# Assigning tokens to tiles by contiguous row groups of x instead of one stride over all of x

## The chip, the cores and the metric

One core of a Trainium2 chip. The metric is the device time of one execution in microseconds (us), lower is better. A median stands for a series of executions; the profile is one further execution, and its span leaves out some 1.3 us of start and end that the time has. A load has landed when the last of its 16 DMA engines has reported. Runs come in two states: a run is called slow when it is over 1.5% above the fastest of its kernel, and only fast runs enter a ratio. All views below are of fast runs with a granted TensorE clock of 1.0 unless the text says otherwise.

## The reference, cut to what matters

```python
# x: [1, 2048, 448] bfloat16; wqkv [448, 1344]; w_phi [16, 28, 28]; wo [448, 448]; w1 [448, 1792]; w2 [1792, 448]
xn = layernorm(x)                       # per token
q, k, v = heads(xn @ wqkv)              # 16 heads of 28
phi_q, phi_k = hedgehog(q @ w_phi), hedgehog(k @ w_phi)   # softmax(+), softmax(-) side by side
attn = (phi_q @ (sum over tokens of phi_k x v)) / (phi_q @ sum of phi_k + 1e-6)
out = x + attn @ wo + silu(xn @ w1) @ w2
```

The 2,048 tokens meet only in the sums over tokens. So any assignment of tokens to the 16 tiles of 128 gives the same result, as long as the load of x and the store of the output agree.

## The kernel before

Five engines run one fixed program each. A small scheduler in the kernel orders it at build time from estimated durations; it looks at the on-chip side of each transfer only. The FFN is the feed-forward part (w1, silu, w2); an eviction copies a result of TensorE out of its accumulators. Parts (cuts marked):

```python
xt = A_x[0].rearrange("(p t) d -> p t d", p=128)      # partition p holds rows 16p .. 16p+15
outt = out[0].rearrange("(p t) d -> p t d", p=128)
...
def load_x(t0, t1):
    load(x_sb[:, t0:t1, :], xt[:, t0:t1, :], f"x{t0}", lat=1400.0)
...
load(Wp[:], ..., "wphi", eng="act")                   # 448 pieces of 56 bytes, ScalarE queue
...
load_x(0, 1); load_x(1, 2); load_x(2, 4)              # sync queue, in this order
load(w1_sb[:, 0:2, 0:512], ..., "w1_0")               # "the first w1 load" below
load(w1_sb[:, 2:4, 0:512], ..., "w1_0r")
load_w1(512, 1024, "act")                             # 384 KB on the ScalarE queue, 128 KB on the sync queue
load_x(4, 8); load_w1(1024, FF); load_rows4(wv_sb, ...)
load_x(8, 12); load_x(12, 16)
...
# the sync queue's order from tile 8 on; wT_dma0..7: transposing loads of the q/k weights from HBM,
# xnT_dma: on-chip transposes of normalised x
chain("x8 wT_dma0 wT_dma1 wT_dma2 x12 xnT_dma5 xnT_dma7 wT_dma3 wT_dma4 wT_dma5 wT_dma6 wT_dma7 xnT_dma9 ...".split())
# VectorE's fixed order of the layer norm: statistics, aggregate, reciprocal, normalise of tiles 0 to 3
chain("bnst0 bnag0 bnst1 bnag1 rstd0 xn0a xn0 rstd1 xn1 bnst2 bnag2 bnst3 bnag3 rstd2 xn2 rstd3 xn3 ev3".split())
# TensorE: transposes tr0, tr1, then FFN pieces of tile 0 ("00a 10a") and tile 1 ("01a 11a"), and so on
...
# the "fold": q/k weights (wT) times the feature weights (BDphi); it needs all eight wT loads
mms += [(wps[:, g, :], wT_sb[0:KP, qk * 4 + g, ...], BDphi[:, g, :], True, True) for g in range(G)]
...
P.dma(lambda e: e.dma_start(out=outt[:, t, cs], in_=res[:, cs]), ..., name="out_dma", ...)
```

The softmax here doesn't subtract the row's maximum and nothing guards it: scores larger than these inputs give would overflow.

Of the kernel before, what the change touches and what calls it, by code (L numbers as in the profile page):

```python
# [344 lines left out]
def bass_parallel_sum__linear_kernel_hedgehog__dense_activation_silu__prompt_kernel(  # L345
# [23 lines left out]
    EPS_DEN = 1e-6  # L369
    NYT = 4  # L370
    XN_DMA0 = 4
    xt = A_x[0].rearrange("(p t) d -> p t d", p=128)
    outt = out[0].rearrange("(p t) d -> p t d", p=128)

    es = contextlib.ExitStack()
    with es:
        def sb(name, shape, dt):
            return es.enter_context(nc.sbuf_tensor(name, shape, dt))

        x_sb = sb("x_sb", [128, NT, D], BF16)  # L380
# [57 lines left out]
        NOS = 4  # L438
# [12 lines left out]
        P = _Prog()  # L451
# [7 lines left out]
        def d_dve(n, mode=1, nptr=0):  # L459
            return n * 1.042 / mode + 160.0 + 30.0 * nptr  # L460
# [38 lines left out]
        def load(dst, src, name, eng="sp", lat=1700.0):  # L499
            n = 2  # L500
            for _, cnt in list(dst.ap):
                n *= cnt
            P.dma(lambda e: e.dma_start(out=dst, in_=src), n / 280.0, writes=[dst], name=name, eng=eng, lat=lat)  # L503
# [5 lines left out]
             reads=[ones_bf[:]], writes=[ident[:]], name="ident")  # L509
# [17 lines left out]
        for i in range(38):  # L527
            P.op("pe", 107.0, lambda e: e.matmul(banks[3][:, 0:128], ones_bf[:], ones_bf[:], start=True, stop=True),
                 reads=[ones_bf[:]], writes=[banks[3][:, 0:128]], name="warm", mode=128)
# [1 line left out]


        def load_x(t0, t1):
            load(x_sb[:, t0:t1, :], xt[:, t0:t1, :], f"x{t0}", lat=1400.0)

        def load_rows4(dst, src, c0, c1, name, eng="sp"):
            load(dst[:, 0:3, :], src[0:KF, c0:c1].rearrange("(k p) f -> p k f", p=128), name, eng)
# [2 lines left out]
        def load_w1(c0, c1, eng="sp"):  # L540
            load_rows4(w1_sb[:, :, c0:c1], B_w1, c0, c1, f"w1_{c0}", eng)

        load_x(0, 1)
        load_x(1, 2)
        load_x(2, 4)
        load(w1_sb[:, 0:2, 0:512], B_w1[0:256, 0:512].rearrange("(k p) f -> p k f", p=128), "w1_0")
        load(w1_sb[:, 2:4, 0:512], bass.AP(B_w1.tensor, B_w1.offset + 256 * FF, [[FF, 128], [64 * FF, 2], [1, 512]]), "w1_0r")
# [246 lines left out]
        ob_cnt = [0]  # L794
# [58 lines left out]
        def out_ev(t, ob, addend, cs):  # L853
            res = x_sb[:, t, :]
            P.op("dve", d_dve(cs.stop - cs.start), lambda e: e.tensor_tensor(res[:, cs], ob, addend[:, cs], ALU.add),  # L855
                 reads=[ob, addend[:, cs]], writes=[res[:, cs]], name="out_ev")
            P.dma(lambda e: e.dma_start(out=outt[:, t, cs], in_=res[:, cs]), 100.0, lat=1200.0, reads=[res[:, cs]], name="out_dma", out_slot=ob_cnt[0] % NOS,
                  eng="sp" if cs.start else "act")
            ob_cnt[0] += 1

# [3 lines left out]
        def finish_tile(t, q, bs):  # L864
            for b, cs in parts(bs):
                ob = banks[b][:, 0:cs.stop - cs.start]
                wo_fulls(q, ob, cs, False)
                P.cur_slack = 400.0
                pe_mms([wo_rem(q, ob, slice(0, 128), cs)], "wo_mm")
                P.cur_slack = 0.0  # L870
                out_ev(t, ob, addend(t), cs)

        def finish_tiles(tiles):
            cs = slice(0, D)
            rows = [[x for x in tiles if x[1] % 2 == i] for i in range(2)]
            tiles = [r[n] for n in range(max(map(len, rows))) for r in rows if n < len(r)]
            pe_mms([wo_rem(q, banks[b][:, 0:D], slice(64 * (q % 2), 64 * (q % 2) + 64), cs) for t, q, b in tiles], "wo_rem",
                   dur=d_mm(D) * max(map(len, rows)), mode=64)
            for t, q, b in tiles:
                out_ev(t, banks[b][:, 0:D], addend(t), cs)  # L880
# [23 lines left out]
        for word in "tr0a tr0 tr1 00a 10a 01a 11a 00b 10b 01b 11b tr2 20 21 tr3 02 12 22 03 13 23".split():  # L904
# [3 lines left out]
            f, t = int(word[0]), int(word[1])  # L908
# [42 lines left out]
        for word in PLAN.split():  # L951
            n0 = len(P.ops)
            kind, arg = word[0], word[1:]
            if kind == "a":
                t, b = map(int, arg[1:].split("@"))
                blocks[arg[0], t] = open_kind[arg[0]](t, b)
                blocks[arg[0], t][2](0)
            elif kind == "b":
                f = blocks[arg[0], int(arg[1:])]
# [5 lines left out]
            elif kind == "K":  # L965
                t0, t1 = map(int, arg.split("-"))
# [9 lines left out]
            elif kind == "U":  # L976
                t, _, b = arg.partition("@")
                att((int(t),), (int(b or UB),))
            elif kind in "FY":
                head, _, cnt = arg.partition(":")  # L980
                t, _, bs = head.partition("@")
                t = int(t)
                if bs:
                    bank_of[t] = [int(c) for c in bs]
                k = done.get(t, 0)
                done[t] = k + int(cnt) if cnt else FT
                if kind == "Y":
                    y_tile(t, bank_of[t][0], k, done[t])
                else:
                    ffn2(t, bank_of[t], False, k, done[t])  # L990
            elif kind == "W":
                t, _, b = arg.partition("@")
                t = int(t)
                if b:
                    bank_of[t] = [int(b)]
                wo_fulls(slot_of[t], banks[bank_of[t][0]][:, 0:D], slice(0, D), t in yts)
            elif kind == "R":
                finish_tiles([(t, slot_of[t], bank_of[t][0]) for t in map(int, arg.split(","))])
            elif kind == "E":
                t = int(arg)  # L1000
                finish_tile(t, slot_of[t], bank_of[t])
            else:
                assert kind == "r"
                t = int(arg)
                P.cur_slack = 400.0
                pe_mms([wo_rem(slot_of[t], banks[bank_of[t][0]][:, 0:D], slice(0, 128), slice(0, D))], "wo_mm")
                P.cur_slack = 0.0
                out_ev(t, banks[bank_of[t][0]][:, 0:D], addend(t), slice(0, D))
# [98 lines left out]
```

## Time and profile before

| | before |
|---|---|
| time, median of 3 | 149.47 us (149.24 to 149.51) |
| span of the profile | 148.2 us |
| TensorE busy | 143.6 us, 97% |
| first FFN matmul | 6.81 us |
| fold begins | 26.38 us |
| last matmul of all begins | 145.90 us |

The prediction below shows the busy shares, the chain, and the head of the timeline. The page also has the span in 40 slices (each 3.7 us; digits are busy tenths, the DMA row is the share of the 16 DMA engines):

```profile
PE   7799999999999999999999999999999999999994
...
DMA  4999955999500000000089570058788467532325
GB/s 101 370 381 211 298 98 97 189 226 347 140 2 4 0 0 7 4 0 4 0 159 168 102 141 4 0 101 172 151 108 176 86 91 144 150 103 51 60 68 184
```

The reader is to see that TensorE is full from the third slice on, and that the second and third slices, 3.7 to 11 us, move 370 to 381 GB/s. The lines of the timeline read:

```profile
6.81 1.81 PE L469 MATMUL psum<-xnT,phT 128*128 128x128 bf16 x24
7.55 0.90 PEld L469 LDWEIGHTS psum<-xnT,phT 128*128 128x128 bf16 x16 [0.31 <-ACT xnT L489]
8.46 0.39 PE L484 MATMUL psum<-ident,RA 128*128 128x128 bf16 x4
...
26.38 0.96 PE L469 MATMUL psum<-BDphi,Y_sb 112*128 112x112 bf16 x16
```

(start, duration, engine, line, operation, out<-in, shapes, count; in the bracket the idle time before it and what ended it). First come the FFN's first 24 matmuls, then the weight load (PEld) at which they pause 0.31 us for tile 1, then the third transpose. The last line is the fold.

### The profile page before, as it was taken

Reading aid. Unit: us, or ns where it says so; the run is one execution under the profiler, and the core shown is the slowest. Engines: PE = TensorE matmul, PEld = TensorE weight load, DVE = VectorE, ACT = ScalarE, POOL = GpSimd, SP = SyncE. Lnnn points to the kernel's source line nnn. Section 1 sums busy time; section 2 is a strip of 40 time slices with the busy share of each in tenths; the row PEclk is TensorE's granted clock in tenths of the full one; section 3 lists DMA queues with packets and bytes.
Section 4 is the critical chain, followed back from the end, with each engine's and each line's share of the span. In section 5 each row is a group of like instructions: output and inputs, shape, how many; then the busy total and the mean of one; then the engine's idle time right before and its main releaser. Section 6 shows DMA issues by size and latency. Waiting matters only on the chain.

```text
span 148.2 us, 3656 instructions
## 1 busy us (share of the span) xinstructions
PE 143.6 (97%) x1540; PEld 79.3 (53%) x1540; DVE 90.3 (61%) x189; ACT 70.7 (48%) x88; POOL 71.4 (48%) x82
## 2 busy tenths in 40 slices
PE   7799999999999999999999999999999999999994
PEld 7594444554554556646444444555545655455573
DVE  1878997541499949504995003999477802915284
ACT  4477757357999399979555859400012000000000
POOL 7108566510079999998799900799000800000000
DMA  4999955999500000000089570058788467532325
GB/s 101 370 381 211 298 98 97 189 226 347 140 2 4 0 0 7 4 0 4 0 159 168 102 141 4 0 101 172 151 108 176 86 91 144 150 103 51 60 68 184
DMA packets 44352, 17.42 MB, mean 117 GB/s; under 512 B 36912, under 2 KB 43952, under 8 KB 44336
## 3 DMA queue, kind: packets, MB, share of 16 engines
q1 hardware_dynamic: 41168, 14.99, 47.7%
q10 hardware_dynamic: 3168, 2.20, 4.8%
q8 instruction: 12, 0.20, 0.6%
q14 instruction: 4, 0.03, 0.1%
HBM read 6.56 MB, written 1.84 MB: 57 GB/s over the span
## 4 chain that ended last, share of the span: by engine, by line
PE 93%; DMA 2%; DVE 2%; ACT 0%; issue 0%; SPq 0%
PE psum L469 93%; DMA x_sb<-in_A_x_dram 2%; DVE RA L617 1%; PE psum L484 1%; DVE x_sb L855 1%; DVE st L602 0%; ACT xnT L489 0%; SPq L503 0%; DVE mv L603 0%; DVE rstd L608 0%
## 5 line engine op out<-in xcount | busy, mean ns | idle before, releaser
L469 PE MATMUL psum<-xnT,phT 64*128 64x512 bf16 (+1 forms) x428 | 45.7, 350 | 0.3
L469 PE MATMUL psum<-w_sb,hT 128*128 128x448 bf16 (+1 forms) x238 | 45.2, 342 | 0.0
L737 DVE TENSOR_REDUCE Rec<-Ek_sb 128x32 f32<-128x896 bf16 (+1 forms) x20 | 24.3, 1246 | 26.8 <-ACT Ek_sb L489 19.2
L773 POOL TENSOR_TENSOR RA<-Ek_sb,Rec 128x896 bf16<-128x896 bf16 x16 | 27.0, 1721 | 21.1 <-DVE Rec L738 19.7
L489 ACT ACTIVATE hT<-psum 128x1024 bf16<-128x1024 f32 x28 | 27.2, 1023 | 13.2 <-PE psum L469 13.2
L469 PEld LDWEIGHTS psum<-w_sb,hT 128*128 128x128 bf16 x238 | 22.3, 98 | 18.7 <-issue 1.5
L469 PEld LDWEIGHTS psum<-xnT,phT 64*128 64x128 bf16 (+1 forms) x428 | 20.8, 95 | 21.1 <-PE psum L469 1.7
L489 ACT ACTIVATE Ek_sb<-psum 128x864 bf16<-128x864 f32 x24 | 20.2, 933 | 17.4 <-DVE x_sb L855 16.1
L469 PE MATMUL psum<-Wqk,xnT 64*128 64x432 bf16 x224 | 23.7, 343 | 0.1
L747 POOL TENSOR_TENSOR Ek_sb<-Ek_sb,Rec 128x896 bf16<-128x896 bf16 x8 | 13.4, 1696 | 9.6 <-ACT phT L489 9.6
L469 PEld LDWEIGHTS psum<-Wqk,xnT 64*128 64x128 bf16 x224 | 10.4, 95 | 10.1 <-PE psum L469 0.8
L747 POOL TENSOR_TENSOR phT<-phT,Rec 128x896 bf16<-128x896 bf16 x8 | 13.4, 1698 | 0.0
L469 PE MATMUL psum<-wv,xnT 64*128 64x448 bf16 x112 | 12.7, 349 | 0.0
L602 DVE BATCH_NORM_STATS2 st<-x_sb 128x6 f32<-128x448 bf16 x16 | 9.7, 604 | 3.6 <-DMA x_sb<-in_A_x_dram 3.6
L469 PE MATMUL psum<-wo_sb,vaug 128*128 128x448 bf16 (+1 forms) x51 | 11.0, 341 | 0.0
L833 DVE TENSOR_SCALAR den<-psum 128x16 f32<-128x16 f32 x16 | 2.4, 156 | 13.4 <-PE psum L469 13.4
L840 DVE TENSOR_TENSOR vaug<-psum,rden 128x448 bf16<-128x448 f32 x16 | 9.8, 622 | 0.4
L489 ACT ACTIVATE vaug<-psum 128x896 bf16<-128x896 f32 x8 | 7.4, 937 | 5.1 <-PE psum L469 5.0
L617 DVE TENSOR_SCALAR RA<-x_sb,mv,rstd 128x384 bf16<-128x384 bf16 (+4 forms) x29 | 8.9, 344 | 1.4 <-POOL rstd L613 1.2
L855 DVE TENSOR_TENSOR x_sb<-psum,x_sb 128x448 bf16<-128x448 f32 (+1 forms) x13 | 7.1, 582 | 2.9 <-PE psum L469 2.9
L738 DVE RECIPROCAL Rec<-Rec 128x32 f32<-128x32 f32 (+1 forms) x24 | 8.5, 391 | 0.1
L469 PEld LDWEIGHTS psum<-wv,xnT 64*128 64x128 bf16 x112 | 5.5, 94 | 5.2
(51 smaller groups left out, 106.3 us busy)
## 6 DMA issues: line engine op xcount, KB each, us to landing
out_dram<-x_sb ACTq DMA_DIRECT2D x15, 112.0 KB, 1.8
w_sb<-in_B_w_dram SPq DMA_DIRECT2D x1, 1568.0 KB, 7.5
x_sb<-in_A_x_dram SPq DMA_DIRECT2D x3, 448.0 KB, 6.1
wo_sb<-in_A_wo_dram SPq DMA_DIRECT2D x2, 336.0 KB, 8.7
phT<-in_B_w_dram SPq DMA_DIRECT2D x1, 576.0 KB, 6.3
phT<-in_B_w_dram SPq DMA_DIRECT2D x2, 256.0 KB, 4.6
phT<-in_B_w_dram ACTq DMA_DIRECT2D x1, 384.0 KB, 4.9
wv<-in_A_wqkv_dram SPq DMA_DIRECT2D x1, 336.0 KB, 6.7
```

The lines of the kernel that those rows point to most:

```text
L469: r = e.matmul(dst, lhsT, rhs, start=st, stop=sp, skip_group_check=True)
L484: r = e.transpose(dst, src, ident[:])
L489: P.op("act", d_act(n), lambda e: e.activation(dst, src, func, scale=scale), reads=[src], writes=[dst], table=table, name=name, **keys)
L602: P.op("dve", 590, lambda e: e.bn_stats(st6[:, t, :], xs), reads=[xs], writes=[st6[:, t, :]], name=f"bnst{t}", okeys_w=["ln"])
L617: P.op("dve", dur, lambda e: e.tensor_scalar(dst, x_sb[:, t, c0:c1], mv[:, t, 0:1], rstd[:, t:t + 1], ALU.subtract, ALU.mult), reads=[xs, ...
L737: P.op("dve", 50 + 967 * n, lambda e: e.tensor_reduce(R2, E4, AXL.X, ALU.add), reads=[E4], writes=[R2], name="Ssum")
L738: P.op("dve", 135 + 210 * n, lambda e: e.reciprocal(R2, R2), reads=[R2], writes=[R2], name="Rrec")
L747: P.op("pool", 1700, lambda e: e.tensor_tensor(E3, E3, Rk[:, :, None].broadcast_to([128, 32, DH]), ALU.mult), reads=[E3, Rk], writes=[E3], ...
L773: P.op("pool", 1700, lambda e: e.tensor_tensor(dst, Eq, Rq.rearrange("p (c j) -> p c j", c=CC)[:, :, :, None].broadcast_to([128, CC, 4, DH ...
L833: P.op("dve", 190, lambda e: e.tensor_scalar(den[:, uq, :], U3[:, :, DH], EPS_DEN, None, ALU.add), reads=[U3[:, :, DH]], writes=[den[:, uq ...
L840: P.op("dve", 620, lambda e: e.tensor_tensor(o3, U3[:, :, 0:DH], rden[:, uq, :, None].broadcast_to([128, H, DH]), ALU.mult), reads=[U3[:, ...
L855: P.op("dve", d_dve(cs.stop - cs.start), lambda e: e.tensor_tensor(res[:, cs], ob, addend[:, cs], ALU.add), reads=[ob, addend[:, cs]], wri ...
```

## The change

The intent: the tiles of a load should be one solid block of x in HBM, instead of 128 pieces 14,336 bytes apart. Tiles 0 and 1 take 128 rows each, tiles 2 and 3 the next 256, then three groups of four tiles with 512 rows. The runs per partition keep their sizes.

```diff
-    xt = A_x[0].rearrange("(p t) d -> p t d", p=128)
-    outt = out[0].rearrange("(p t) d -> p t d", p=128)
+    TILES = ((0, 1), (1, 2), (2, 4), (4, 8), (8, 12), (12, 16))
+
+    def rows_of(a, t0, t1):
+        for u0, u1 in TILES:
+            if u0 <= t0 < u1:
+                v = a[0][128 * u0:128 * u1, :].rearrange("(p t) d -> p t d", p=128)
+                return v[:, t0 - u0:t1 - u0, :]
@@
-            load(x_sb[:, t0:t1, :], xt[:, t0:t1, :], f"x{t0}", lat=1400.0)
+            load(x_sb[:, t0:t1, :], rows_of(A_x, t0, t1), f"x{t0}", lat=1400.0)
@@
-            P.dma(lambda e: e.dma_start(out=outt[:, t, cs], in_=res[:, cs]), ...
+            P.dma(lambda e: e.dma_start(out=rows_of(out, t, t + 1)[:, 0, cs], in_=res[:, cs]), ...
```

More of the change, by code (lines that the diff above doesn't have):

```diff
@@ L856, in out_ev @@
                  reads=[ob, addend[:, cs]], writes=[res[:, cs]], name="out_ev")
-            P.dma(lambda e: e.dma_start(out=outt[:, t, cs], in_=res[:, cs]), 100.0, lat=1200.0, reads=[res[:, cs]], name="out_dma", out_slot=ob_cnt[0] % NOS,
+            P.dma(lambda e: e.dma_start(out=rows_of(out, t, t + 1)[:, 0, cs], in_=res[:, cs]), 100.0, lat=1200.0, reads=[res[:, cs]], name="out_dma", out_slot=ob_cnt[0] % NOS,
                   eng="sp" if cs.start else "act")
```

## The prediction

> **What bounds the kernel now.** I read four things in this order: the busy shares, the chain of work that ended last, the timeline of the first ten microseconds, and the DMA share of that same stretch.
>
> The busy shares say which engine can matter:
>
> ```profile
> PE 143.6 (97%) x1540; PEld 79.3 (53%) x1540; DVE 90.3 (61%) x189; ACT 70.7 (48%) x88; POOL 71.4 (48%) x82
> ```
>
> TensorE is busy 143.6 of 148.2 us. Only 4.6 us of the span are not TensorE work, and a change that leaves every matmul alone can touch nothing else. Busy is not the same as useful: 38 warm-up matmuls (3.9 us) are in it too. So the chain is asked next where the useful work begins:
>
> ```profile
> 0.80 0.41 SPq L503
> 1.21 0.06 issue
> 1.27 3.10 DMA x_sb<-in_A_x_dram
> 4.37 0.02 issue
> 4.40 0.64 DVE st L602
> ...
> 5.32 0.58 DVE RA L617 x2
> ...
> 6.01 0.41 DVE RA L617
> 6.42 0.05 issue
> 6.47 0.41 PE psum L484 x4
> 6.88 0.02 issue
> 6.90 0.60 ACT xnT L489
> 7.51 0.05 issue
> 7.55 1.07 PE psum L469 x16
> ...
> 35.10 110.69 PE psum L469 x1184
> ```
>
> (columns: start us, duration us, what). The chain is a head of about 7.5 us and then TensorE to 145.8 without a break worth naming. The head starts with the second load of x (tile 1, issued at 1.27, landed at 4.37), then layer-norm statistics, normalise, transpose on TensorE, eviction on ScalarE, first FFN matmuls of tile 1. The load of x is the only piece of the chain that the change touches, apart from the stores at the very end.
>
> How tight the head is, the timeline shows:
>
> ```profile
> 3.18 0.63 DVE L602 BATCH_NORM_STATS2 st<-x_sb 128x6 f32<-128x448 bf16 x1 [3.18 <-DMA x_sb<-in_A_x_dram]
> 3.84 0.18 DVE L603 BATCH_NORM_AGGREGATE mv<-st 128x2 f32<-128x6 f32 x1
> 4.40 0.63 DVE L602 BATCH_NORM_STATS2 st<-x_sb 128x6 f32<-128x448 bf16 x1 [0.37 <-DMA x_sb<-in_A_x_dram]
> 6.33 0.62 DVE L602 BATCH_NORM_STATS2 st<-x_sb 128x6 f32<-128x448 bf16 x1
> ```
>
> VectorE works in a fixed order here. It has tile 0's statistics done at 3.84 + 0.18 = 4.02 and then stands idle 0.37 us for tile 1. Tile 2's statistics at 6.33 have no wait in front of them. These 0.37 us are the prize that is visible without any assumption.
>
> Last, how well the first loads use the DMA engines (columns: stretch, length, busy of five engines, granted clock, DMA share, GB/s):
>
> ```profile
> 2.00:2.50 0.50, 0.50 (x7) 0.50 (x6) 0.00 (x0) 0.50 (x1) 0.50 (x2) 1.00 0.89 195
> 2.50:3.00 0.50, 0.50 (x8) 0.50 (x6) 0.00 (x0) 0.24 (x2) 0.34 (x4) 1.00 1.40 220
> 3.00:3.50 0.50, 0.50 (x8) 0.50 (x6) 0.32 (x1) 0.00 (x0) 0.38 (x3) 1.00 0.67 156
> 3.50:4.00 0.50, 0.50 (x7) 0.50 (x6) 0.47 (x2) 0.00 (x0) 0.50 (x1) 1.00 1.01 353
> ```
>
> From 2.0 to 3.5 us, when tiles 0 and 1 arrive, the rate is 156 to 220 GB/s; from 3.5 us on, with weights, it is 353 and more. The share is nevertheless high, so packets are long in flight rather than missing. The packet records say the same: the median 896-byte packet takes 41 ns, but between 2.5 and 3.0 us the mean is 77 ns and the longest 951 ns. The 16 engines report tile 0 between 2.59 and 3.15 us, and tile 1 between 3.20 and 4.37 us, the last three at 3.96, 4.09 and 4.37: a few stragglers decide when tile 1 counts as landed.
>
> **What the Trainium skill says.** The page DMA: Bandwidth & Descriptors, section "Anatomy of one DMA", puts about 2.0 us of a DMA down to fixed cost, most of it the receipt from the target, and only the rest to bytes (a fit for the other descriptor path). The trace roughly agrees: tile 0 needs 2.35 us for 112 KB, tile 1 needs 3.1 us for the same bytes, so at most 0.3 to 1.1 us can depend on where the rows lie. Section "Latency and other measured facts" of that page gives HBM access as 0.2 us on average and 2 us at high load; packets of 41 ns beside one of 951 ns show such a spread. The same section has a row pitch that slows copies only from 512 KiB up, by an inferred aliasing of channels; the pitch here is 14,336 bytes, so it is no proof for this case. Section "How a descriptor splits into AXI transactions" charges a start that is not 256-byte aligned with extra beats: by its rule every row of the old tile 1 costs 32 beats instead of 28, as does half the rows of tiles 0 and 1 afterwards. The trace does not show it: 41 ns is the median while either tile arrives.
>
> **The change, part by part.**
> 1. Instructions. The order listings of both kernels agree on all five engines, entry for entry, with the same waits and shapes. No matmul, eviction, statistic or DMA is added or removed; the scheduler reads only the on-chip side. Cost 0.
> 2. Loads of x. Six loads, same bytes, same contiguous runs (896, 896, 1,792 and three of 3,584 bytes per partition). Only the pitch between partitions changes: 16 rows x 896 = 14,336 bytes for every load before; afterwards each load is one solid block (pitch 896, 896, 1,792, 3,584). Tile 0 used to take 128 separated pieces spread over 1.8 MB; now it takes 112 KB in one piece.[...] If tile 1's spread of 1.18 us shrinks to the 0.56 us of tile 0, it lands near 3.20 + 0.56 = 3.76 us; for tile 0 I allow 0.1 us.
> 3. What of that reaches the path. Tile 1's statistics can start at the later of 3.76 + 0.03 and the end of tile 0's aggregate, 4.02 - 0.1 = 3.92. That is 0.48 us before the present 4.40. Then three limits come up together. Tile 2 landed at 5.96 by its completion records, and its statistics would be wanted at 6.33 - 0.48 = 5.85: cap 0.37 us unless it too is earlier. The first w1 load landed at 6.68 and its first user begins at 6.78; moved up to 6.73, eight matmuls of about 55 ns (1.81 us for 24, with a 0.31 us wait inside, gives about 60) end near 7.2, where tile 1's matmuls now begin at 7.55: cap 0.35 us. The TensorE idle between warm-up end (4.97) and first transpose (5.82) is 0.85 us and no cap. I take 0.35 us.
> 4. Loads 8 to 16 of tiles. They already run at 353 to 395 GB/s and have slack: tiles 4 to 7 are in well before VectorE turns to them at 10.12. On the path 0.
> 5. Stores. Same sizes: 896 bytes per row and two halves of 448. The pitch falls from 14,336 to 3,584 bytes or less. Fifteen hide under TensorE; the last pair lands in 1.6 us after issue, most of it fixed. 0, give or take 0.1.
>
> Sum: -0.35 us, carried through a TensorE that never again waits for long. 149.47 - 0.35 = 149.12, say 149.1 us.
>
> **The rivals.**
> - Weights take over. Were x much earlier but the weights not, w1 at 6.68 keeps the gain at 0.35. For: the first user follows the landing by 0.10 us. Against: the weights queue behind x and might move up as well. If everything moves, w1 included, the gain could reach the 0.85 us of TensorE idle: about 148.6.
> - Nothing happens. The stragglers could be cold accesses that any first load pays, wherever the rows lie; the w1 packets in the same stretch also reach 499 ns. Then 149.4 to 149.5.
> - It gets worse. Sixteen engines walking one small block might meet in the same HBM parts and wait in turn. Against it: the old walk had all engines a common multiple of 14,336 bytes apart[...]. About 149.7 to 150.
> - The stores slow or speed the end: up to 0.2 us, since only the last pair is exposed.
>
> **Range and chances.** Centre 149.1. The runs of before spread 149.24 to 149.51, and the no-effect case belongs in the range, so the top is 149.6; the all-moves case is the bottom, 148.55. Two per cent is 3.0 us; the whole head before the first useful FFN matmul is 6.8 us and the load of x only 3.1 of it, most of that fixed. Nothing I see gains or loses 3 us: chances 0.01 faster, 0.98 same, 0.01 slower.
>
> **What would show it.** Right: in the chain, the piece of the x load issued at 1.27 shrinks from 3.10 to about 2.5 us; the 0.37 us idle before the second statistics vanishes; the GB/s of 2.0 to 3.5 us rise; tile 1's first FFN matmuls start near 7.2 instead of 7.55; everything behind is displaced by a constant, and the TensorE busy stays 143.6 within 0.3. If x lands early but the 7.55 does not move, the weights took over, and the first 128-wide matmuls will show a DMA wait. Wrong: the same landing at 4.37, or an end that moves by more than the start of the FFN does. Then a store or a later wait, which I put at zero, is what changed.

## The result, and the profile after

| | before | after |
|---|---|---|
| median of 4 | 149.49 us (149.24 to 149.67) | 149.80 us (149.54 to 149.95) |
| span of the profile | 148.2 us | 148.7 us |
| tile 0 / tile 1 of x landed | 3.15 / 4.37 us | 3.06 / 3.73 us |
| tiles 2 and 3 landed | 5.96 us | 6.25 us |
| first w1 load landed | 6.68 us | 7.00 us |
| first FFN matmul | 6.81 us | 7.14 us |
| third transpose on TensorE | 8.46 us | 8.48 us |
| last transposed q/k weight load landed | 25.79 us | 26.68 us |
| fold begins | 26.38 us | 26.82 us |
| last matmul begins | 145.90 us | 146.34 us |

The ratio is 1.002, with a 95% interval of 1.000 to 1.0041. A ratio is the mean time of one kernel's fast runs over that of the other's of the same rounds, so it is not quite the ratio of the medians. Nothing moved by 2%; the time lies 0.2 us above the predicted range.

The VectorE timeline of the changed kernel, tile by tile, where 4.40 us had been tile 1's statistics:

```profile
3.85 0.59 DVE L608 BATCH_NORM_STATS2 st<-x_sb 128x6 f32<-128x448 bf16 x1
...
6.27 0.63 DVE L608 BATCH_NORM_STATS2 st<-x_sb 128x6 f32<-128x448 bf16 x1 [0.44 <-DMA x_sb<-in_A_x_dram]
```

Tile 1 came when the prediction said (3.73 against 3.76 us), and its statistics began 0.55 us earlier than before. But the wait of 0.37 us in front of tile 1 only moved: there are now 0.44 us in front of tile 2. The windows show the DMA rate while this happens (columns as in the prediction):

```profile
2.50:3.00 0.50, 0.50 (x8) 0.50 (x6) 0.00 (x0) 0.24 (x2) 0.34 (x4) 1.00 1.27 241
3.00:3.50 0.50, 0.50 (x8) 0.50 (x6) 0.41 (x1) 0.00 (x0) 0.43 (x3) 1.00 0.68 162
3.50:4.00 0.50, 0.50 (x7) 0.50 (x6) 0.47 (x3) 0.00 (x0) 0.50 (x1) 1.00 0.96 279
4.00:4.50 0.50, 0.50 (x8) 0.50 (x6) 0.47 (x2) 0.29 (x1) 0.27 (x1) 1.00 0.98 319
```

The rate rose a little where tiles 0 and 1 arrive (241 against 220 GB/s from 2.5 to 3.0 us, 162 against 156 after that, though 185 against 195 before it), and fell behind them (279 against 353 GB/s from 3.5 to 4.0 us). The TensorE timeline then shows both places where the time went:

```profile
7.14 1.50 PE L475 MATMUL psum<-xnT,phT 128*128 128x128 bf16 x24 [0.64 <-ACT xnT L495]
8.48 0.39 PE L490 MATMUL psum<-ident,RA 128*128 128x128 bf16 x4
...
26.82 0.95 PE L475 MATMUL psum<-BDphi,Y_sb 112*128 112x112 bf16 x16 [0.36 <-DMA Y_sb<-in_A_wqkv_dram]
```

First, the FFN starts 0.33 us later than before, not earlier. The bracket names ScalarE's eviction, but that is the inference of the view: the first of these matmuls belongs to tile 0, whose eviction had ended at 6.30 us. The first w1 load landed at 7.00 us, and the matmul followed 0.14 us later, as it had followed by 0.13 us before (6.68 and 6.81). Once started, its 24 matmuls ran without a break, where before they had paused for tile 1; the third transpose is therefore level with before. Second, at the fold TensorE waits for the transposed weight loads. Up to there the two kernels differ by 0.02 us; from there on by 0.44 us. The chain of work that ended last has changed accordingly (start, duration, what):

```profile
0.80 2.27 DMA x_sb<-in_A_x_dram
...
20.22 1.26 SPq L566
...
21.52 2.30 SPq L566
...
23.86 2.83 DMA Y_sb<-in_A_wqkv_dram
26.68 0.14 issue
26.82 8.66 PE psum L475 x94
```

The chain now runs through the sync queue's transposing loads, one of which held the queue for 2.30 us where the four others of the last five took 1.26, and reaches TensorE at the fold. The last weight load was issued 1.15 us later than before (23.86 against 22.71 us). About half of that is this hold, since one load of the kernel before held the queue too, for 1.71 us; the other half is an on-chip transpose ahead of them that held it for 1.94 instead of 1.39 us.

My theory after this reading (A): the place of the rows decides when the loads land, tile 1 for the better and the rest for the worse. The rival (B): landings scatter from one execution to the next, and two profiles of two kernels had been compared as if they were the kernels.

### The profile page after: what moved, and what is told of

It reads as the page before. It is cut to its first block, busy times and chain, and to the rows that moved or that the text cites. A ratio compares the mean times of both kernels' runs of the same rounds, so it can differ in the third digit from the quotient of the medians.

```text
span 148.7 us, 3656 instructions
## 1 busy us (share of the span) xinstructions
PE 144.2 (97%) x1540; PEld 79.8 (54%) x1540; DVE 90.2 (61%) x189; ACT 71.1 (48%) x88; POOL 71.3 (48%) x82
## 4 chain that ended last, share of the span: by engine, by line
PE 82%; DVE 6%; SPq 4%; DMA 3%; issue 1%; POOL 1%; ACT 0%; DVEq 0%
PE psum L475 82%; SPq L566 4%; DVE st L608 3%; DMA Y_sb<-in_A_wqkv_dram 2%; DVE RA L623 2%; DMA x_sb<-in_A_x_dram 2%; DVE mv L609 1%; PE psum L490 1%; DVE x_sb L861 1%; ACT xnT L495 0%; POOL rstd L619 0%; DVE xnT L499 0%; POOL ve L617 0%; DVE rstd L614 0%; DVEq L1071 0%
```

## The experiments

The table collects every fast profile of a full kernel; the four "head" kernels have their own table further down. The record names the chip of these runs (8, then 6, 1 and 5; none for the first pair), so two profiles may differ by the chip as well as by the execution. "Reaches fold" is the start of the first v matmul plus 9.03 us, the time that the TensorE work between the two takes where nothing waits; "weights + 0.14" is the landing of the last transposed q/k weight load plus the 0.14 us until its user starts. All in us.

| profile | x rows | tile 1 | tiles 2, 3 | first w1 | FFN starts | reaches fold | weights + 0.14 | fold starts | last matmul |
|---|---|---|---|---|---|---|---|---|---|
| before | old | 4.37 | 5.96 | 6.68 | 6.81 | 26.38 | 25.93 | 26.38 | 145.90 |
| before, again | old | 4.09 | 5.83 | 6.57 | 6.70 | 26.10 | 26.22 | 26.21 | 145.72 |
| stores only | old | 4.08 | 5.83 | 6.58 | 6.72 | 26.09 | 26.36 | 26.36 | 145.86 |
| before, queue order | old | 4.23 | 6.46 | 7.67 | 7.81 | 27.07 | 25.89 | 27.06 | 146.58 |
| after | new | 3.73 | 6.25 | 7.00 | 7.14 | 26.40 | 26.82 | 26.82 | 146.34 |
| after, third | new | 3.74 | 6.44 | 7.21 | 7.34 | 26.60 | 26.29 | 26.59 | 146.12 |
| loads only | new | 4.11 | 6.17 | 6.76 | 6.90 | 26.23 | 26.64 | 26.63 | 146.27 |
| after, queue order | new | 4.10 | 6.17 | 6.97 | 7.11 | 26.37 | 25.21 | 26.36 | 145.88 |

Three things are read from it. The FFN starts 0.13 to 0.14 us after the first w1 load in all eight, whatever tile 1 does. The fold starts at the later of the two columns before it, within 0.01 us in all eight. And the last matmul begins 119.51 to 119.64 us after the fold, so that the kernel's end is settled by then. The rule for the fold was read off five of these profiles; the third run of after and the two with the new queue order came later and obeyed it.

### Both kernels once more

No edit. The kernel before against itself:

> The kernel before, unchanged, run against itself: the control. Every theory expects a ratio of 1.000 with an interval that holds 1.000. What it is for is a second profile. Theory A (the place of the rows of x decides when the loads land): tile 1 lands near 4.37 us again, tiles 2 and 3 near 5.96, the first w1 load near 6.68, and the last of the eight transposed loads of the q/k weights near 25.8, so that TensorE does not wait for it at the fold. Theory B (the landings scatter from run to run whatever the kernel): at least one of these four moves by 0.3 us or more from the first profile, and the fold wait of 0.36 us seen after the change may appear here too.

Measured: correct, ratio 0.9991 (0.9949 to 1.0033). Runs in the fast state ranged from 149.13 to 149.96 us, those of before in the same rounds from 149.29 to 151.21 (to 150.67 at a granted clock of 1.0). The VectorE and TensorE timelines:

```profile
4.11 0.63 DVE L602 BATCH_NORM_STATS2 st<-x_sb 128x6 f32<-128x448 bf16 x1 [0.16 <-DMA x_sb<-in_A_x_dram]
```

```profile
6.70 1.64 PE L469 MATMUL psum<-xnT,phT 128*128 128x128 bf16 x24
8.17 0.39 PE L484 MATMUL psum<-ident,RA 128*128 128x128 bf16 x4
...
26.21 0.95 PE L469 MATMUL psum<-BDphi,Y_sb 112*128 112x112 bf16 x16
```

The unchanged kernel has here what was promised of the change: tile 1's statistics 0.29 us earlier (4.11 against 4.40), the third transpose 0.29 us earlier (8.17 against 8.46). By the fold 0.17 us of it are left (26.21 against 26.38), because the last transposed weight load landed at 26.08 us instead of 25.79 and TensorE, due at 26.10, started 0.13 us after the landing. None of the four landings moved by the full 0.3 us that I had set for theory B (the largest differences are 0.28 us for tile 1 and 0.29 us for the last weight load), so strictly its mark was missed by a hair. But a difference of the size predicted, and of the size to be explained, lies between two executions of one kernel.

The changed kernel again:

> The changed kernel, unchanged, once more. Theory A: ratio 1.001 to 1.004 again; tile 1 near 3.73, tiles 2 and 3 near 6.25, the first w1 load near 7.00, last transposed q/k weight load near 26.7, and a TensorE wait of about 0.36 us for it at the fold. Theory B: tile 1 may stay early, but the stragglers of tiles 2 and 3 and of w1 and the fold wait come and go; if the fold wait is absent in this profile its span is some 0.4 us shorter than 148.7.

Measured: correct, ratio 0.9971 (0.9934 to 1.0007), median 149.27 against 149.56 us. Its profile fell in the slow state (granted clock 0.989); it is no support for A, for tile 1 landed at 4.38 us in it. The sign of the first result (1.002) has turned.

And a third time:

> The changed kernel a third time, because its second profile fell in the slow state. From the five fast profiles so far: TensorE starts the fold at the later of (start of its first v matmul + 9.03 us) and (landing of the last transposed q/k weight load + 0.14 us), and its last matmul starts 119.5 us after that. This run must obey that sum within 0.1 us whatever its landings are. If the change places the landings, tile 1 lands near 3.7 us again; if they scatter, anything from 3.7 to 4.4.

Measured: correct, ratio 0.9998 (0.9936 to 1.0061). The sum of the table held: 17.57 + 9.03 = 26.60, fold at 26.59 us, last matmul 119.52 us later. Tile 1 landed at 3.74 us again. This time the view names the right releaser at the start of the FFN, because no eviction ended beside it:

```profile
7.34 1.50 PE L475 MATMUL psum<-xnT,phT 128*128 128x128 bf16 x24 [1.01 <-DMA phT<-in_B_w_dram]
```

(the tile named phT also holds w1 at this time). And there is no wait at the fold here. Over three series of the changed kernel the ratios are 1.002, 0.997 and 1.000.

### Loads alone, stores alone

Fragments of the lines that differ from the changed kernel:

```diff
 # loads only: new groups for the loads, old stride for the stores
-out=rows_of(out, t, t + 1)[:, 0, cs]
+out=out[0].rearrange("(p t) d -> p t d", p=128)[:, t, cs]
 # stores only: old stride for the loads, new groups for the stores
-rows_of(A_x, t0, t1)
+A_x[0].rearrange("(p t) d -> p t d", p=128)[:, t0:t1, :]
```

> New row groups for the loads of x, old stride for the stores (a wrong result on purpose, rows come out permuted). If the loads alone cause the difference (my theory), the ratio is that of the whole change, 1.001 to 1.004, and the landings of the head are those of the changed kernel. If the stores cause it, the ratio is 1.000 and the last store's end and the stores' landing times are those of before.

> Old stride for the loads of x, new row groups for the stores (a wrong result on purpose). If the loads alone cause the difference: ratio 1.000 and landings in the head as before (tile 1 near 4.37 us). If the stores cause it: ratio 1.001 to 1.004, with TensorE ending at about 145.9 as before and the difference behind it.

Measured (both wrong results): loads only 0.9985 (0.9949 to 1.0022), stores only 1.0006 (0.9959 to 1.0052). The times decide nothing: the intervals hold both theories' values. The profiles say more. With the stores alone changed the span ends 2.3 us after the start of the last matmul (148.2 and 145.86), as before (148.2 and 145.90): the stores' pitch shows nothing at the end. And stores only, with the old loads, waits at the fold, which had looked like a mark of the change:

```profile
26.36 0.95 PE L475 MATMUL psum<-BDphi,Y_sb 112*128 112x112 bf16 x16 [0.20 <-DMA Y_sb<-in_A_wqkv_dram]
```

My expectation that loads only would show the landings of the changed kernel failed for tile 1: 4.11 instead of 3.73 us. On the chip of these rounds that is level with the old rows (4.09 and 4.08 us). Nor is a long hold of the queue a mark of the change: with the old loads, stores only had one of 2.31 us.

### The disputed load by itself

A kernel with nothing in it but single tiles: load one at the old pitch, wait, load one as a solid block, wait, 16 pairs from two tensors of x's size; then stores in turns.

```python
for t in range(8):
    one(x_sb[:, t, :], strided(A_x, t))     # one(): start, then wait for completion
    one(b_sb[:, t, :], block(B_x, t))
# then 8 pairs with the tensors exchanged, then 8 pairs of stores
```

> The disputed cost by itself: nothing but tiles of 128 rows x 896 bytes, each loaded and waited for alone, in turns once at the old pitch of 14,336 bytes and once as a solid block; then stores in turns in both forms (a wrong result on purpose). If the pitch decides how fast a tile lands, the blocks land faster by 0.3 us or more on the mean of 16 pairs, in the first half and in the second alike. If it does not, the two means differ by less than 0.1 us, and the first load of each tensor is the only slow one.

Measured (one look, state unknown, clock 1.0; wrong result on purpose): from start of issue to the last engine's report, old pitch 1.97 and 1.95 us in the two halves, solid block 1.91 and 1.94 us. Over all 16 pairs 1.96 against 1.93 us. The stores took 1.66 and 1.67 us. The issue times of the sync queue show the same even steps:

```profile
4.64 0.33 SPq L19 DMA_DIRECT2D x_sb<-in_A_x_dram  x1
6.53 0.33 SPq L19 DMA_DIRECT2D b_sb<-in_B_x_dram  x1
8.46 0.33 SPq L19 DMA_DIRECT2D x_sb<-in_A_x_dram  x1
```

A tile alone hardly cares where its rows lie (0.03 us), and no load was slow for being the first of its tensor. Yet in the kernel before, the same tile needed 2.35 (tile 0) and 3.10 us (tile 1). What is added there must come of the company.

### Taking the wait at the fold away

```diff
-wT_dma0 wT_dma1 wT_dma2 x12 xnT_dma5 xnT_dma7 wT_dma3 wT_dma4
+wT_dma0 wT_dma1 wT_dma2 wT_dma3 xnT_dma5 xnT_dma7 x12 wT_dma4
```

The fourth transposed load goes out while the sync queue is idle, and the load of tiles 12 to 15 takes its place. TensorE's program is unchanged.

> Kernel before, with the fourth transposed q/k weight load issued where the load of tiles 12 to 15 stood and that load behind the second on-chip transpose; the sync queue stands idle 2 us there. Should bring the last transposed q/k weight load from 25.8 to 26.2 us down by about 0.7 us, to near 25.3. If the fold's wait is what holds the end, there is no wait at the fold, the fold starts 9.03 us after the first v matmul, and the kernel gains what it waited before: 0 to 0.3 us, ratio 0.998 to 1.000. If something else holds it: no change or a later wait.

> Changed kernel with the same reordering. If the fold's wait of 0.3 to 0.4 us is where the gain of the head (if any) went, it disappears, and the ratio to before is 0.996 to 0.999, 0.3 us better than the change alone; its last matmul starts 128.5 us after its first v matmul. If the change itself costs time elsewhere, it stays at or above 1.000.

Measured: both correct; ratios 1.0004 (0.9938 to 1.0071) and 1.0006 (0.9939 to 1.0074). In both the fold starts 9.02 to 9.03 us after the first v matmul, without a wait. The last weight load landed at 25.75 and 25.07 us. For the kernel before, 25.3 us had been expected, and its fold would have waited for nothing in any case, because TensorE came late (27.07 us); so the evidence is the changed kernel's. The TensorE timeline of the changed kernel with this order:

```profile
7.11 1.50 PE L475 MATMUL psum<-xnT,phT 128*128 128x128 bf16 x24 [0.51 <-DMA phT<-in_B_w_dram]
...
26.36 0.96 PE L475 MATMUL psum<-BDphi,Y_sb 112*128 112x112 bf16 x16
```

Against the first profile of the changed kernel, which reached the same point at the same time (26.40 and 26.37), this one is 0.46 us ahead at the fold and at the last matmul (145.88 against 146.34). That the wait at the fold cost this in that execution is shown. That the new order gains in the median is not: the rounds scattered by nearly 2 us (fast runs of before from 149.16 to 151.00, to 150.77 at a granted clock of 1.0), and in the profile of the kernel before with this order the first w1 load came at 7.67 us and took everything back.

### Taking the crowd away

"Head": with the queue order above, the 384 KB of w1 go from the ScalarE queue to the sync queue, behind the first w1 loads. "Head2": the 56-byte pieces of the feature weights go behind the load of tiles 4 to 7 as well.

```diff
-load_w1(512, 1024, "act")
+load_w1(512, 1024)
 # head2 only: load(Wp[:], ..., "wphi", eng="act") moved behind load_x(4, 8), on the sync queue
```

> Kernel before with the reordering of before_swap, and the 384 KB load of w1's columns 512 to 1023 taken off the ScalarE queue and put behind the first w1 loads on the sync queue. In all eight profiles so far the first FFN matmul starts 0.13 to 0.14 us after the first w1 load lands (6.57 to 7.67 us), never after tile 1. If the ScalarE-queue load is what delays it and tiles 2 and 3, both land about 1 us earlier (w1 near 5.8, tiles 2 and 3 near 5.0), the FFN starts when tile 0's eviction allows, near 6.3, and the end gains 0.3 to 0.5 us (ratio 0.997). If the loads are late for another reason, nothing moves by more than 0.2 us.

> The changed kernel with the same two edits: w1 is no longer the gate, so an earlier tile 1 can show. If the new row groups bring tile 1 forward (3.7 against 4.2), this kernel's third transpose and first v matmul are 0.2 to 0.4 us earlier than those of before_head. If the row groups do nothing (as for the loads measured alone: 1.93 against 1.96 us), they are the same within 0.1 us.

> before_head with the load of the 28 x 28 feature weights (448 pieces of 56 bytes, issued on the ScalarE queue at 0.80 us, beside tile 0) moved behind the load of tiles 4 to 7 as well. If crowding by other loads is what makes tiles 0 and 1 need 2.3 and 2.9 us where a tile alone needs 1.95, both land earlier: tile 0 near 2.8, tile 1 near 3.4 to 3.6, and less scatter of tile 1. If the rows' places are what makes them slow, tile 1 stays at 4.1 to 4.4 here.

> The changed kernel with all three edits. Crowding theory: tile 0 and tile 1 land as in before_head2 within 0.15 us, and so does everything after them; ratio of the two to each other 1.000. Row-place theory: tile 1 lands 0.3 us or more before that of before_head2.

Measured, all correct:

| | ratio to before | tile 0 | tile 1 | tiles 2, 3 | first w1 | FFN starts | third transpose | first v matmul |
|---|---|---|---|---|---|---|---|---|
| before + head | 1.0039 (0.9994 to 1.0084) | 3.10 | 3.58 | 5.64 | 6.34 | 6.47 | 7.92 | 17.27 |
| after + head | 1.0004 (0.9957 to 1.0050) | 2.91 | 3.94 | 4.73 | 5.45 | 6.27 | 8.03 | 17.23 |
| before + head2 | 1.0059 (1.0012 to 1.0106) | 2.78 | 3.76 | 5.07 | 5.79 | 6.09 | 7.85 | 18.06 |
| after + head2 | 1.0088 (1.0042 to 1.0135) | 2.83 | 3.29 | 4.37 | 5.14 | 5.98 | 8.30 | 18.50 |

The crowd theory is right about the direction of the landings, though in the first row w1 came at 6.34 us where about 5.8 was expected, and still set the FFN's start: with the old rows, tile 1 lands at 3.58 and 3.76 us once the 384 KB are gone, against 4.08 to 4.37 with them; without the 56-byte pieces tile 0 lands at 2.78 us, against 3.05 to 3.15 with them. It also frees the FFN's start, down to 5.98 us, and the third transpose. But I expected a gain of 0.3 to 0.5 us at the end, and there is none. The TensorE timeline of the kernel before with head2 tells why:

```profile
6.09 0.61 PE L469 MATMUL psum<-xnT,phT 128*128 128x128 bf16 x8
...
7.85 0.39 PE L484 MATMUL psum<-ident,RA 128*128 128x128 bf16 x4
9.34 0.34 PE L469 MATMUL psum<-xnT,phT 128*128 128x128 bf16 x3 [1.10 <-DMA phT<-in_B_w_dram]
```

The w1 columns that were pushed back are now the gate, with 1.10 us of waiting; the first v matmul is 0.7 and 1.15 us later than the 17.35 us of the first profile of before. In "head" the same gate costs 0.20 us and the first v matmul stays where it was. In these four kernels, what came earlier in the head was paid for by the loads behind it. That is not all that head2 lost: in both its profiles the span ends 3.28 us after the start of the last matmul instead of 2.35. The last store goes out 0.4 us later after that start and takes 0.5 us longer to land. Why, no run here shows. The two pairs disagree on the rows of x (tile 1: 3.58 old and 3.94 new, then 3.76 old and 3.29 new), so this left open whether the row groups act on tile 1 at all.

### The loads of the head, 48 times in one program

```python
for kind in ORDER:      # O, N: old and new rows with the two ScalarE-queue loads; o, n: without them
    # both queues wait for all loads of the group before
    # sync queue: tile 0, tile 1, tiles 2-3, w1_0, w1_0r, w1_512r; ScalarE queue: Wp, w1_512
```

> The loads of the kernel's head alone, 48 times over in one program, each group waited for before the next (a wrong result on purpose): 24 groups with the two ScalarE-queue loads beside the six of the sync queue, 24 without; half of each with the old pitch and half with the new row groups, in balanced order. Still open is whether the new row groups bring tile 1 forward when other loads crowd it (fast profiles of the full kernels: old 4.09 to 4.37, new 3.73 to 4.11). If the place matters under crowding, tile 1's mean of 12 lands 0.2 us or more earlier with the new groups while the ScalarE-queue loads run; if not, the two means differ by less than 0.1 us and the scatter within one layout (0.2 us and more) covers what the full kernels showed. In either case tile 1 without the ScalarE-queue loads should land 0.3 us or more earlier than with them.

Measured (one look, state unknown, clock 1.0; wrong result on purpose), means of 12 in us from the group's first issue to landing, with the standard deviation in brackets:

| | tile 0 | tile 1 | tiles 2, 3 | first w1 | last of the six |
|---|---|---|---|---|---|
| crowded, old rows | 2.21 | 3.53 (0.32) | 5.22 (0.24) | 6.05 (0.36) | 7.06 |
| crowded, new rows | 2.15 | 3.11 (0.37) | 5.36 (0.26) | 6.16 (0.32) | 7.19 |
| alone, old rows | 1.98 | 2.55 (0.11) | 3.74 (0.30) | 4.57 (0.29) | 6.06 |
| alone, new rows | 1.97 | 2.54 (0.17) | 3.56 (0.17) | 4.37 (0.12) | 6.02 |

This answers it, for one execution on one chip. The new row groups do bring tile 1 forward where it is crowded, by 0.42 us (standard error 0.14, from the two deviations over 12 samples each). Without the ScalarE-queue loads they do nothing to it (0.01 us). And what tile 1 gains in the crowd is not passed on: tiles 2 and 3 and the first w1 load are 0.14 and 0.11 us later with the new rows, at standard errors of 0.10 and 0.14. With the company gone they are 0.18 and 0.20 us earlier with the new rows, some two standard errors, but the last load is level there too (6.06 and 6.02), and the kernels do not have that case. Tile 1's deviation of 0.3 us within one layout explains why single profiles contradicted each other. The full kernels agree in direction: tile 1 lands at 4.19 us in the mean of the four profiles with old rows, at 3.92 with new. Where the extra wait of a crowded old-pitch load arises inside the memory or the DMA engines, no run here shows. One rival is left untested: the change also moves where rows start. If x begins on a 256-byte boundary, every row of the old tile 1 starts 128 bytes off one, and half of the new ones do. The median 896-byte packet took 41 ns in all four kinds of group, which does not speak for it.

## Why the prediction was wrong

- **That nothing but the loads of x and the stores is touched, and that the stores cost nothing** held: both profiles count 3,656 instructions, and stores only ended 2.3 us behind its last matmul as before.
- **Tile 1 lands near 3.76 us** held in direction and about in size: 3.73 us in the first profile, 0.42 us of gain in the mean of the crowded loads. But rows in one place hardly load faster in themselves (1.93 against 1.96 us alone); in the crowd test they suffered less from the two loads on the ScalarE queue. The prediction's estimate that 0.3 to 1.1 us could depend on the rows' place took a fixed cost of 2.0 us off each load; but a whole load alone took less than that, and in the crowd test the company cost tile 1 0.98 us, of which the new rows saved 0.42. Its 41 ns are the recorded time of one packet, far below even the average latency that it set beside them, so they neither confirm nor deny that latency. And it read the low GB/s of the first stretch as x's, where 448 pieces of 56 bytes were in flight too. And the 4.37 us that it started from was the latest of four old-row landings (4.08 to 4.37): part of the prize was an unlucky execution.
- **"I take 0.35 us"** is the step that failed. It kept the first w1 load at 6.68 us and let its user move up to 6.73. In all eight profiles the FFN starts 0.13 to 0.14 us after that load, so this was no cap of 0.35 us on the start but the gate itself; only the pause of 0.31 us for tile 1 behind it could be won. The repeated kernel before was 0.29 us ahead at the third transpose without any change: 0.17 us of the pause (1.64 against 1.81 us for the 24 matmuls) and 0.11 us from an earlier w1 load. In the first profile of the changed kernel the load landed 0.33 us later, and the pause that was saved went into that: third transpose 8.48 against 8.46 us. That the new rows make this load later is not shown (0.11 us at a standard error of 0.14 in the crowd test). The rival "weights take over" named the mechanism, but still credited it with the full 0.35 us.
- **"A TensorE that never again waits for long"** failed too. With the old queue order the fold starts 0.13 to 0.59 us after the last transposed weight load; in five of the six profiles with the old queue order the room ("reaches fold" less "weights + 0.14") was under 0.35 us or negative, so the full gain could not have gone through unless these loads had moved up as well. The prediction had read one profile, the only one with more room (0.45 us by the table). In the first profile of the changed kernel this wait cost the 0.4 us that made that execution slower; the prediction's own sign for it, an end that moves by more than the FFN's start (0.44 against 0.33 us), did show.
- **The range.** The measured 149.80 us lies above 149.6. The range took its width from three runs of before within 0.27 us; fast runs of the same kernel later ranged from 149.12 to 151.21 us, and to 150.77 at a granted clock of 1.0. Three series give 1.002, 0.997 and 1.000: there is no gain or loss larger than this scatter, and a change of 0.1 to 0.2% in either direction remains undecided.

## What to carry to other kernels

Before a late landing is called a property of a layout, take a second profile of the unchanged kernel and load the thing alone: here the first showed most of the "gain" for nothing, and the second showed no gain without neighbours. Where the head of a kernel is a full DMA stream, ask which transfer the first matmul waits for, not which one the chain of one execution names; bringing another one forward did not move that one here. And follow a small gain to every later meeting of TensorE with a load: while that load stays where it is, the slack there is the most that can arrive at the end (0.45 us in the first profile, 0.31 us or none in the other five).

## What the Trainium skill lacked or had wrong

- DMA: Bandwidth & Descriptors, section "Latency and other measured facts", gives copy rates for row pitches from 512 KiB up. No page has a small pitch: at 14,336 bytes a 112 KB tile alone loads in 1.96 us against 1.93 us as a solid block, but beside two loads of the other queue in 3.53 against 3.11 us.
- The same page, section "Issuing engines are not separate DMA queues", says that transfers of different issuers interleave on the same engines. It does not say how much a small load suffers by it: tile 1 went from 2.55 to 3.53 us with the old rows, the first w1 load from 4.57 to 6.05 us.
- The same page, section "How a descriptor splits into AXI transactions", charges starts that are not 256-byte aligned. At the old pitch, if the tensors begin aligned, odd tiles start 128 bytes off and even tiles do not. Loaded alone, the odd ones took 1.92 us and the even ones 2.00 us: no such charge shows there; in a crowd it was not tested apart.
- No page tells in microseconds how long a transposing load of this size holds the queue that issues it: 1.26 us for four of the last five, 2.30 us for one in the changed kernel (2.31 us for one with the old loads in stores only), which had its part in turning a slack of 0.45 us at the fold into a wait.
